# Turning q and k of the first row blocks one tensor at a time, with less MoE work while batch 0 runs

## Chip, cores, metric

One core of a Trainium2 chip. The metric is the device time of one execution, in microseconds (us). A profile gives one execution with a record of every instruction; its span is some 1.8 us shorter than the time of the same execution (352.4 and 354.17 for the profiled execution of the kernel before).

## The reference, cut

Causal attention with a forget gate, 8 batches x 8 heads, 576 rows, head size 64, then a two-layer MoE block (one expert here) with SiLU on the 4608 rows of 512 that come out.

```python
def _attn_ref(q, k, v, f):                     # q, k, v: (8, 8, 576, 64); f: (8, 8, 576)
    scores = scale * np.matmul(q, k.transpose(0, 1, 3, 2))
    cum = np.cumsum(np.log(np.clip(f, 0.0001, 1.0)), axis=-1)
    decay = cum[:, :, :, None] - cum[:, :, None, :]
    scores = np.where(causal, -1000000000.0, scores + decay)
    ...                                        # softmax
    return np.matmul(attn, v)

def _moe_ref(x, w_in, w_out):                  # x: (4608, 512), w_in: (512, 2048), w_out: (2048, 512)
    h = x @ w_in
    g = h * (1.0 / (1.0 + np.exp(-h)))
    return (g @ w_out).astype(np.float32)
```

## The kernel before

The first 128 rows of each of the 8 batches ("blocks 0 to 7") are done first, since each needs only its own 128 keys. Blocks 0 to 3 form MoE group 0 (512 rows), blocks 4 and 5 group 1, blocks 6 and 7 group 2 (256 rows each). Then comes the loop over the remaining rows: batch 0, batch 1 and so on, each in four units of two heads; two units make a "pair". ( `u` below is the exponential of a unit's scores, `ut` that of its tail, the last 64 rows.) Program order is the order of issue on every engine.

A block is turned (q and k transposed by matmuls into PSUM, q evacuated by the scalar engine, ACT, and k by the vector engine, DVE), scored, masked, multiplied with v, normalised and turned back:

```python
    def load_qk0(b):
        t = conv.tile([P, 2, RUN * D], BF16, name="qkb", tag="qkb")     # conv: 4 buffers
        for i, src in enumerate((q, k)):
            nc.gpsimd.dma_start(out=t[:, i, :], in_=src[b, :, 0:P, :].rearrange(...))
        qk0[b] = t

    def turn0(b, between=0):
        src = qk0.pop(b)
        qT0[b] = qktp.tile([P, NP, P], BF16, name="qkT", tag="qkT")
        for i, (dst, evac) in enumerate(
            ((qT0[b], nc.scalar.copy), (kT0[b], nc.vector.tensor_copy))
        ):
            ...                       # 16 matmuls into tp, then evac(dst, tp)
```

For the remaining rows the software engine (POOL) casts a loaded unit to bf16, and a transposing DMA turns it.

```python
    def cast_qk(n):
        b, p = divmod(n, NP)
        t2 = conv.tile([P, NX, 2 * D], BF16, name="qkb", tag="qkb")
        ...                           # three POOL casts
        qbf[n] = t2

    def transposes(n):
        src = qbf.pop(n)
        t = qktp.tile([P, NX, P], BF16, name="qkT", tag="qkT")
        ...
        nc.sync.dma_start_transpose(out=t[:, :, :], in_=src[:, :, :].rearrange("p x c -> p (x c)"))
```

MoE work lies between all this in pieces: `m1_chunk` (first layer: four matmuls, a tanh on ACT, a product `gt` on DVE) and `m2_part` (second layer: four matmuls of 512 columns; the last part of a row block sends its output by the sync queue). `fill` issues pieces until a budget is spent; what it overdraws is carried in `at["left"]` to the next call. `least` is a minimum number of pieces whatever the account says.

```python
    def fill(us_, first=0, least=0):
        ...
        at["left"] += us_ * 1000
        while at["left"] > 0 or least > 0:
            t = step()                # one chunk or one part; returns its estimated ns
            if t is None:
                at["left"] = 0.0
                return False
            at["left"] -= t
            least -= 1
        return True

    def two_more(b):
        turn0(b)
        fill(0.6, 0, 1)
        turn0(b + 1)
        fill(0.6, 0, 1)
        scores0(b)
        mask0(b)
        fill(0.6, 2, 1)
        ...

    fill(4.0)
    two_more(4)
    ready.add(1)
    fill(6.0)
    open2["w"] = True                 # the second layer may begin
    fill(5.0, 2)
    two_more(6)
    ready.add(2)
    fill(1.0, 2)

    def prepare(n):                   # issues on the sync queue (SP) and on POOL
        if n + 4 < NU:
            load_qk(n + 4)
        if n + 2 < NU:
            cast_qk(n + 2)
            transposes(n + 2)
        ...                           # v of the next batch

    for m in range(NQ):
        n = 2 * m
        piece = 1.4 if m < 2 else 2.4
        scores(n, 0)
        scores(n, 1)
        prepare(n)
        slot(piece, 2)                # = fill(piece, 2) and some bookkeeping
        ...
        attend(n)
        attend(n + 1)
        slot(min(3.5, max(0.8, behind() - LAG)), 1)
```

The softmax here doesn't subtract the row's maximum and nothing guards it: scores larger than these inputs give would overflow.

## Time and profile before

| what | value |
|---|---|
| time, median of 3 (later 4) | 354.05 (354.06) us, 353.91 to 354.12 |
| tensor engine (PE) idle in the span | 15.6 us of 352.4 |
| PE waiting on transposed q and k | none among the ten largest waits |
| first MoE matmul | 20.65 us |
| first chunk of group 1 | 40.45 us |
| batch 0 begins | 61.12 us |

The three times of the lower rows are starts of matmuls in the PE timeline; I use them as mile marks. A change that removes idle time moves the later marks forward, if the work before them is the same; where it isn't, its duration has to be taken off first (four matmuls of 512 columns are 0.865 us, four of 256 are 0.44).

### The profile page before, as it was taken

To read this page: it belongs to the slowest core of one execution; us is meant where nothing else is said; L and a number is where in the kernel's file an instruction comes from. 1 tells how busy PE (TensorE), PEld (TensorE's weight loads), DVE (VectorE), ACT (ScalarE), POOL (GpSimd) and SP (SyncE) were. 2 spreads that over 40 slices of the span, in tenths; PEclk is the share of its full clock that TensorE was granted. 3 is DMA by queue.
4 is the path that set the end of the run, shared out by engine and by line. 5 is a ranking of instruction groups with operands and counts; after the bars stand their busy time and mean duration, and the time that the engine had idled before them with its cause. 6 is when DMAs were issued, how large, how long until landed. Compare 5 with 4: busy or idle time off the path is not lost.

```text
span 352.4 us, 8990 instructions
## 1 busy us (share of the span) xinstructions
PE 336.8 (96%) x3598; PEld 203.7 (58%) x3646; DVE 188.8 (54%) x409; ACT 218.3 (62%) x399; POOL 103.2 (29%) x183
## 2 busy tenths in 40 slices
PE   7888988999899999999999999999999999999995
PEld 3544554666656566565665666756566565555664
DVE  4566824456566465656656546646556544444340
ACT  5555716785766867759658675676856744444341
POOL 6992146254062144127017115412600000000000
PEclk9999999999999999999999999999999999999999
DMA  8999999998865795699279389848722000010012
GB/s 159 215 200 201 196 192 196 213 211 182 188 135 110 184 206 120 105 209 197 74 150 230 75 186 211 169 99 183 159 58 58 32 32 30 30 61 31 32 60 60
DMA packets 138969, 47.92 MB, mean 136 GB/s; under 512 B 127984, under 2 KB 134384, under 8 KB 138928
## 3 DMA queue, kind: packets, MB, share of 16 engines
q1 hardware_dynamic: 132240, 40.93, 55.9%
q0 software_dynamic: 6528, 6.29, 10.8%
q8 instruction: 28, 0.46, 0.5%
q10 hardware_dynamic: 160, 0.13, 0.1%
q14 instruction: 13, 0.11, 0.1%
HBM read 36.85 MB, written 9.44 MB: 131 GB/s over the span
## 4 chain that ended last, share of the span: by engine, by line
PE 89%; ACT 3%; DVE 2%; issue 2%; DMA 2%; POOL 1%; POOLq 0%; ACTq 0%
PE po L570 35%; PE hp L532 34%; PE sc L433 7%; PE dn L478 5%; PE dn L487 3%; PE tx L508 2%; DMA qkb<-in_k_dram 2%; PE tp L271 2%; ACT u L312 1%; DVE gt L541 1%; ACT u L437 1%; POOL qkb L124 1%; DVE xq L350 1%; ACT th L540 1%; PE sc L305 1%
## 5 line engine op out<-in xcount | busy, mean ns | idle before, releaser
L541 DVE SCALAR_TENSOR_TENSOR gt<-th,hp 128x384 bf16<-128x384 bf16 (+2 forms) x208 | 106.0, 522 | 79.8 <-ACT th L540 76.5
L540 ACT ACTIVATE th<-hp 128x384 bf16<-128x384 f32 (+2 forms) x208 | 95.5, 475 | 85.7 <-PE hp L532 82.9
L532 PE MATMUL hp<-x,w_in_bf 128*128 128x384 bf16 (+2 forms) x829 | 145.9, 314 | 2.6 <-DVE gt L541 0.8
L570 PE MATMUL po<-w_out_bf,gt 128*128 128x512 bf16 (+1 forms) x550 | 139.3, 374 | 3.2 <-issue 1.6
L532 PEld LDWEIGHTS <-w_in_bf 128*128 128x128 bf16 x832 | 78.9, 98 | 56.6 <-issue 3.2
L570 PEld LDWEIGHTS <-gt 128*128 128x128 bf16 x592 | 54.2, 98 | 48.7 <-issue 2.5
L437 ACT ACTIVATE u<-sc 128x1024 bf16<-128x1024 f32 (+1 forms) x96 | 74.6, 814 | 10.7 <-PE sc L433 10.1
L387 POOL TENSOR_TENSOR vp<-vf,w_bf 128x520 bf16<-128x520 f32 (+1 forms) x32 | 34.0, 1063 | 45.3 <-DMA vf<-in_v_dram 43.0
L442 DVE TENSOR_TENSOR u<-u,tri 128x768 bf16<-128x768 bf16 x32 | 21.8, 681 | 22.5 <-ACT u L437 22.5
L373 POOL CAST qkb<-qf 128x384 bf16<-128x384 f32 x32 | 17.1, 535 | 54.7 <-DMA qf<-in_q_dram 49.9
L579 ACT ACTIVATE osb<-po 128x512 f32<-128x512 f32 (+1 forms) x37 | 22.0, 593 | 16.2 <-PE po L570 15.8
L456 DVE TENSOR_TENSOR ut<-ut,trit 128x128 bf16<-128x128 bf16 x32 | 9.3, 291 | 33.3 <-ACT ut L449 33.3
L433 PE MATMUL sc<-qkT 64*128 64x128 bf16 (+1 forms) x640 | 26.5, 207 | 0.1
L433 PEld LDWEIGHTS <-qkT 64*128 64x128 bf16 x640 | 18.2, 94 | 8.8 <-issue 5.8
L449 ACT ACTIVATE ut<-sc 128x640 bf16<-128x640 f32 x32 | 22.8, 714 | 0.0
L478 PEld LDWEIGHTS <-u 128*128 128x128 bf16 x576 | 20.7, 97 | 2.7 <-issue 0.2
L478 PE MATMUL dn<-vp,u 128*128 128x65 bf16 x384 | 21.8, 194 | 0.0
L496 DVE TENSOR_TENSOR xr<-dn,rec 128x448 bf16<-128x448 f32 x32 | 20.0, 624 | 1.1
L373 POOL CAST qkb<-kf 128x384 bf16<-128x384 f32 x32 | 16.6, 519 | 11.5 <-DMA kf<-in_k_dram 11.3
L478 PE MATMUL dn<-v,u 128*128 128x65 bf16 x192 | 19.8, 194 | 0.0
L377 POOL CAST qkb<-qktf 128x128 bf16<-128x128 f32 x32 | 10.6, 333 | 21.3 <-DMA qktf<-in_k_dram 21.3
L433 PE MATMUL sc<-qkT,kT 64*128 64x64 bf16 (+1 forms) x128 | 16.0, 258 | 0.0
(64 smaller groups left out, 191.1 us busy)
## 6 DMA issues: line engine op xcount, KB each, us to landing
vf<-in_v_dram SPq DMA_DIRECT2D x32, 256.0 KB, 4.9
out_dram<-osb SPq DMA_DIRECT2D x32, 256.0 KB, 2.3
qf<-in_q_dram SPq DMA_DIRECT2D x64, 96.0 KB, 2.9
kf<-in_k_dram SPq DMA_DIRECT2D x64, 96.0 KB, 2.7
w_in_bf<-in_moe_w_in_dram POOLq DMA_DIRECT2D x4, 512.0 KB, 9.9
w_out_bf<-in_moe_w_out_dram POOLq DMA_DIRECT2D x4, 512.0 KB, 13.5
qkb<-in_q_dram POOLq DMA_DIRECT2D x8, 128.0 KB, 7.1
qkb<-in_k_dram POOLq DMA_DIRECT2D x8, 128.0 KB, 7.4
```

What stands on the lines that cost most here:

```text
L373: nc.gpsimd.tensor_copy(out=t2[:, c0 : c0 + NR, :].rearrange("p c x -> p (c x)"), in_=t[:, :, :, :].rearrange("p c h d -> p (c h d)"),)
L387: nc.gpsimd.tensor_tensor(out=vbf[b][r, c, :, :], in0=vst[b][c][r, :, :], in1=w_bf[r, c + 1, b * H : (b + 1) * H, None].to_broadcast([n, H ...
L433: nc.tensor.matmul(sc[:, i, o : o + q1 - q0], lhsT=kt, rhs=t[r, q0:q1], start=True, stop=True)
L437: nc.scalar.activation(out=u[:, :, c * SM : c * SM + w], in_=sc[:, :, 0:w], func=ACT.Exp, scale=scale)
L442: nc.vector.tensor_tensor(out=x, in0=x, in1=tri[:, None, None, :].to_broadcast([P, 2, NR, P]), op=ALU.mult,)
L449: nc.scalar.activation(out=ut[:, :, 0:3:2, :].rearrange("p k i t -> p i k t"), in_=sc[:, :, T0 : T0 + (NM + 1) * ST].rearrange("p i (k t) ...
L478: nc.tensor.matmul(dn[:, i * NR + c - 1, :], lhsT=u[:, i, o : o + P], rhs=vals(kb, i), start=(kb == 0), stop=(kb == c),)
L532: nc.tensor.matmul(hp[:, :], lhsT=w_in_bf[:, cc, fc * P : (fc + 1) * P], rhs=xg(g)[:, cc, :], start=(cc == 0), stop=(cc == NCC - 1),)
L540: nc.scalar.activation(out=th[:, :], in_=hp[:, :], func=ACT.Tanh, scale=0.5)
L541: nc.vector.scalar_tensor_tensor(out=gt[:, fc, :], in0=th[:, :], scalar=1.0, in1=hp[:, :], op0=ALU.add, op1=ALU.mult,)
L570: nc.tensor.matmul(po[:, :], lhsT=gt[:, fc, tb * P : (tb + 1) * P], rhs=w_out_bf[:, fc, m0:m1], start=(fc == 0), stop=(fc == NFC - 1),)
L579: nc.scalar.activation(out=osb[:, :], in_=po[:, :], func=ACT.Copy, scale=0.5)
```

## The change

Its intent: start the MoE work earlier by filling the first twenty microseconds better (turn one tensor at a time, hold v of blocks 2 and 3 back behind k of block 0, finish block 3 in two halves), lay more chunks beside blocks 6 and 7, and in exchange put less MoE work into batch 0.

```diff
-    for b in range(4):
-        load_v0(b)
+    load_v0(0)
+    load_v0(1)
+    after(qk0[0][0:1, 1, 0:16])        # the sync queue waits for k of block 0
+    load_v0(2)
+    load_v0(3)
...
-    def turn0(b, between=0):           # both tensors
-        src = qk0.pop(b)
+    def turn0(b, i):                   # one tensor
+        src = qk0[b]
...                                     # out0 and back0 can work in halves
-    turn0(1)
-    sc = ban0(0)
-    scores0(0, sc)
-    turn0(2)
-    sc = ban0(1)
-    scores0(1, sc)
+    turn0(1, 0)
+    turn0(1, 1)
+    scores0(0, ban0(0))
+    scores0(1, ban0(1))
...
-    keep_warm(2)
-    out0(3)
-    back0(2, on_dve)
-    keep_warm(2)
-    back0(3, on_act)
+    keep_warm(1)
+    out0(3, 1)
+    back0(2, on_act)
+    back0(3, on_act, on_dve)
...
     def two_more(b):
-        turn0(b)
-        fill(0.6, 0, 1)
-        turn0(b + 1)
-        fill(0.6, 0, 1)
+        for x in range(2):
+            for i in range(2):
+                turn0(b + x, i)
+                fill(0.3, 0, x == 1 or i == 1)
...
-        fill(1.6, 2, 1)
+        fill(2.4, 2, 3)
...
-        fill(0.8, 0, 1)
+        fill(0.8, 0, 2)
...
-    fill(5.0, 2)
+    fill(3.0, 2)
     two_more(6)
     ready.add(2)
-    fill(1.0, 2)
...
-    LAG = 12.0
+    LAG = 13.0
...
-        piece = 1.4 if m < 2 else 2.4
+        piece = 1.3 if m < 2 else 2.4
...
-        slot(min(3.5, max(0.8, behind() - LAG)), 1)
+        slot(min(3.5, max(0.8, behind() - LAG)) if m > 1 else 0.8, 1)
```

More of the change, by code (lines that the diff above doesn't have):

```diff
@@ L258 @@
     u0: dict[int, bass.AP] = {}
-    def turn0(b, between=0):
-        src = qk0.pop(b)
-        qT0[b] = qktp.tile([P, NP, P], BF16, name="qkT", tag="qkT")
-        for i, (dst, evac) in enumerate(
-            ((qT0[b], nc.scalar.copy), (kT0[b], nc.vector.tensor_copy))
-        ):
-            if i == 1 and between:
-                keep_warm(between)
-            tp = pbig.tile([P, NP, NRUN, RUN], FP32, name="tp", tag="big")
-            for c in range(RUN):
-                for j in range(2):
-                    nc.tensor.matmul(
-                        tp[j * D : (j + 1) * D, :, :, c].rearrange("p a r -> p (a r)"),
-                        lhsT=src[:, i, c * D : (c + 1) * D],
-                        rhs=sel[:, j, :],
-                        start=True,
-                        stop=True,
-                    )
-            evac(
-                out=dst[:, :, :].rearrange("p a t -> p (a t)"),
-                in_=tp[:, :, :, :].rearrange("p a r c -> p (a r c)"),
-            )
+    def turn0(b, i):
+        src = qk0[b]
+        if i == 0:
+            qT0[b] = qktp.tile([P, NP, P], BF16, name="qkT", tag="qkT")
+        dst, evac = ((qT0[b], nc.scalar.copy), (kT0[b], nc.vector.tensor_copy))[i]
+        tp = pbig.tile([P, NP, NRUN, RUN], FP32, name="tp", tag="big")
+        for c in range(RUN):
+            for j in range(2):
+                nc.tensor.matmul(
+                    tp[j * D : (j + 1) * D, :, :, c].rearrange("p a r -> p (a r)"),
+                    lhsT=src[:, i, c * D : (c + 1) * D],
+                    rhs=sel[:, j, :],
+                    start=True,
+                    stop=True,
+                )
+        evac(
+            out=dst[:, :, :].rearrange("p a t -> p (a t)"),
+            in_=tp[:, :, :, :].rearrange("p a r c -> p (a r c)"),
+        )
     def ban0(b):
@@ L333, with out0 @@
     xqs: dict[int, bass.AP] = {}
-    def out0(b):
+    def out0(b, step_=2):
         dn = psc.tile([P, 2, 4, P], FP32, name="dn0", tag="sc")
@@ L349, in out0, with back0 @@
         xq = xqp.tile([P, H, D], BF16, name="xq", tag="xq")
-        nc.vector.tensor_tensor(
-            out=xq[:, :, :].rearrange("p (g j) d -> p g j d", g=2),
-            in0=dn[:, :, :, 0:D],
-            in1=rec[:, :, :, None].to_broadcast([P, 2, 4, D]),
-            op=ALU.mult,
-        )
+        for g in range(0, 2, step_):
+            nc.vector.tensor_tensor(
+                out=xq[:, 4 * g : 4 * (g + step_), :].rearrange("p (g j) d -> p g j d", j=4),
+                in0=dn[:, g : g + step_, :, 0:D],
+                in1=rec[:, g : g + step_, :, None].to_broadcast([P, step_, 4, D]),
+                op=ALU.mult,
+            )
         xqs[b] = xq
-    def back0(b, copy):
+    def back0(b, *copies):
         xq = xqs.pop(b)[:, :, :].rearrange("p (c j) d -> p c (j d)", j=2)
-        tx = pbig.tile([P, NCC, P], BF16, name="tx", tag="big")
-        for cc in range(NCC):
-            nc.tensor.transpose(tx[:, cc, :], xq[:, cc, :], ident_bf[:, :])
         g, c0 = HEADS_OF[b]
-        copy(out=xg(g)[:, :, c0 : c0 + P], in_=tx[:, :, :])
+        k = NCC // len(copies)
+        for n, copy in enumerate(copies):
+            tx = pbig.tile([P, k, P], BF16, name="tx", tag="big")
+            for cc in range(k):
+                nc.tensor.transpose(tx[:, cc, :], xq[:, n * k + cc, :], ident_bf[:, :])
+            copy(out=xg(g)[:, n * k : (n + 1) * k, c0 : c0 + P], in_=tx[:, :, :])
     def cast_qk(n):
@@ L649 @@
     weights_scan()
-    turn0(0, between=3)
+    turn0(0, 0)
+    keep_warm(3)
+    turn0(0, 1)
     nc.vector.tensor_scalar(
@@ L672 @@
     load_v0(4)
+    turn0(2, 0)
+    turn0(2, 1)
     out0(0)
-    turn0(3)
-    sc = ban0(2)
-    scores0(2, sc)
+    turn0(3, 0)
+    scores0(2, ban0(2))
     convert_v0(2)
     load_v0(5)
+    turn0(3, 1)
     out0(1)
     back0(0, on_dve)
-    sc = ban0(3)
-    scores0(3, sc)
+    scores0(3, ban0(3))
     convert_v0(3)
```

## The prediction

> **What bounds the kernel now.** I read the page first (engine shares, the chain that ended last), then the tensor engine's busy time stage by stage, then what it waited for, then the order of instructions of both built programs on each engine.
>
> ```profile
> span 352.4 us, 8990 instructions
> PE 336.8 (96%) x3598; PEld 203.7 (58%) x3646; DVE 188.8 (54%) x409; ACT 218.3 (62%) x399; POOL 103.2 (29%) x183
> PE 89%; ACT 3%; DVE 2%; issue 2%; DMA 2%; POOL 1%; POOLq 0%; ACTq 0%
> ```
>
> The tensor engine is busy for 336.8 of 352.4 us and no other engine passes 62%. The change removes three warm-up matmuls and no other tensor work, so the time can only move by what happens to the 15.6 us in which that engine stands idle. Where they lie, stage by stage (first column the stretch, second its length, third the tensor engine's busy time):
>
> ```profile
> 0.00:20.60 20.60, 16.32 (x235) 9.36 (x239) 10.58 (x25) 11.26 (x14) 17.37 (x42) 1.00 1.09 188
> 20.60:40.40 19.80, 18.45 (x167) 8.97 (x170) 13.58 (x23) 12.72 (x22) 9.21 (x13) 1.00 1.23 200
> 40.40:61.10 20.70, 18.52 (x190) 11.22 (x190) 9.88 (x21) 9.56 (x20) 9.50 (x15) 1.00 1.08 195
> 61.10:69.30 8.20, 7.78 (x128) 5.19 (x130) 2.84 (x8) 6.67 (x11) 2.30 (x5) 1.00 0.88 212
> 84.40:100.70 16.30, 15.36 (x182) 10.14 (x183) 8.82 (x23) 10.66 (x21) 4.90 (x9) 1.00 0.88 187
> 100.70:340.00 239.30, 237.03 (x2464) 142.95 (x2495) 131.19 (x286) 154.13 (x284) 52.53 (x90) 1.00 0.53 115
> 340.00:352.40 12.40, 8.51 (x61) 5.79 (x60) 1.54 (x4) 3.01 (x7) 0.00 (x0) 1.00 0.23 64
> ```
>
> Idle is 4.3 us before the first MoE matmul (1.2 of it the start), 1.35 while blocks 4 and 5 run, 2.2 while 6 and 7 run, 0.4 in the first pair of batch 0 (61.1 to 69.3), 0.9 in the third (a wait of 0.8 at 91.4), 2.3 over the next 239 us, 3.9 after the last matmul. The change touches the first five: at most about 8 us, 2% of the time. What those idle times wait for:
>
> ```profile
> PE dn L340 <- DVE u L321: 1.5, 3, 0.6
> PE hp L532 <- DVE kT L278: 0.8, 1, 0.8
> PE hp L532 <- ACT x L364: 0.7, 1, 0.7
> PE tp L271 <- DMA qkb<-in_q_dram: 0.6, 1, 0.6
> PE tp L271 <- DMA qkb<-in_k_dram: 0.5, 2, 0.4
> PE tx L362 <- DVE xq L350: 0.5, 2, 0.4
> PE sc L286 <- ACT u L312: 0.5, 1, 0.5
> ```
>
> These are latencies of masks, evacuations and loads with too little tensor work laid beside them. The DMA share is above 1 in every slice up to 61 us.
>
> **What the Trainium skill says.** "TensorE: Matmul & The Clock Gate", Back-to-back issue gap: a warm matmul of N columns takes N/2.4 + 2.5 ns, 216 ns for 512. The trace agrees: the first 20 of 512 columns take 4.48 us with the drain of the last. So I count 0.865 us for four of 512 columns and 0.44 for four of 256. The same page, Why this matters for your kernels, wants no idle gap over about 3 us lest the clock fall. The longest single wait here is 1.2 us and the granted clock is 1.00 in these stages; the pauses that I expect below are about 1 us each, so I count no clock loss, also not from three fewer warm-ups. "DMA: Bandwidth & Descriptors", Queues, rings and completion order: each DMA engine takes turns between its queues. The trace agrees: from 9 to 12 us the software queue (q, k, weights) moved 0.45 MB while the hardware queue (v) moved 0.15. Holding v back can therefore only re-order a saturated stream. "Perfetto Trace Analysis", Optimization Strategy, advises interleaving regimes with different limits; the change does so more in one place and less in another.
>
> **The change part by part.** I carry durations of the trace through the new order: turning one tensor (16 matmuls) 0.51 us, exponential of a block about 1.0, evacuation of q 0.58 and of k 0.69, mask 0.69, reciprocal and product 0.9.
>
> *Held v.* By 7 us the hardware queue has moved 0.67 MB, which is f, v of block 0 and of block 1; blocks 2 and 3 had hardly begun when k of block 0 landed (6.75). So q0, k0 and q1 (8.4) gain nothing; q2 and k2 come perhaps 0.8 us earlier, v2 and v3 some 0.3 later.
>
> *The first four blocks.* The exponential of block 1 no longer waits behind turning block 2: it starts at about 11.5 and not 12.76. Carried on, the exponential of block 3 starts at about 16.0 (17.04), the last product is split in halves, and the first MoE matmul starts at about 19.0 (20.65): 1.65 us, with 0.65 of warm-up matmuls in it. The first quarter of the input weights has landed by then (18.3).
>
> *Blocks 4 and 5.* Here most of it is lost again. q of block 5 lands at about 26.6 (issued 16.75, 9.8 to landing), and the stream is saturated, so it does not come earlier. The tensor engine would be there at 25.3: it waits 1.3. The next MoE chunk takes the PSUM bank of that q, whose evacuation must wait for the scores of block 4 (only one buffer for it is free): 0.6. Six chunks later the sixteenth is done before block 5 comes back, so nothing lies beside its copy: 0.7 more. Against that, the two mask waits (0.7) vanish. The first chunk of group 1 starts at about 39.9 instead of 40.45: 0.5 us ahead.
>
> *Blocks 6 and 7.* Three chunks instead of two lie between masks and outputs, two between outputs and turning back, and single tensors are turned between chunks, in banks that the built program gives free in time. All 2.1 us of waits should go. Other small gaps: 0.5. In all the tensor engine is some 3.1 us ahead in work when batch 0 begins.
>
> *The first pair of batch 0.* Counting chunks in the built orders, the kernel after has by then done 5 first-layer chunks of 256 (2.2 us) and 4 second-layer parts (3.5 us) more. The minimum counts of the fills overdraw their account by 4.1 us, so the first pair gets no chunk at all among its scores and attention (4 parts and 2 chunks before, 4.3 us). What is left there is 3.7 us of tensor work, against the scalar engine's 0.5 for an output plus 5.7 for exponentials (two pairs of 0.95 each, and 0.27 + 0.6 for each tail). With two score buffers the tensor engine follows it: about 7.0 us for 3.7 of work, a loss of 3.3, in pauses of about 1 us; 3.2 net of the 0.1 before.
>
> *The third pair.* Five first-layer chunks in a row cost 0.8 us before because the second layer had run out. After, chunks and parts alternate there: 0.8 gained.
>
> *Transposed q and k.* The third output DMA now stands in the sync queue ahead of the loads of block 4. It is ready about 1.3 us after batch 0 begins, and the queue was contiguous before:
>
> ```profile
> 60.76 1.70 SPq L583 DMA_DIRECT2D out_dram<-osb  x2
> 62.51 1.04 SPq L150 DMA_DIRECT2D qf<-in_q_dram  x2
> ...
> 78.22 1.25 SPq L401 DMA_TRANSPOSE qkT<-qkb  x1
> ```
>
> From the loads at 62.5 to the transpose at 78.2 it needs 15.2 us without the two outputs between, and 3.2 to landing. It would land 18 to 20 us after the batch's start; the third pair now comes after 7.0 + 0.9 + 9.4 = 17.3. That is a wait of 0.7 to 2.5 unless the freer stream speeds the issues (v loads took 1.0 us each here, 0.75 at 94 us). I enter 0.7.
>
> Sum: -3.1 + 3.2 - 0.8 + 0.7 = 0.0. The tuning of such small constants was probably judged by measurements, so I shade it a little down: 353.8 us.
>
> **Rivals.** (1) The earlier start is kept: the wait on q5 is smaller, since by 9 us more of the software queue is done, and pauses in the first pair are filled better than I think: 350.5 to 352. For it: q5's landing is read from another mix of traffic. Against it: the saturated share. (2) The transposes bind: third pair, then the second half of it wait, 2 to 3 us: 356. For it: the contiguous sync queue. Against it: the loads had spare time in later pairs. (3) The overdrawn account costs nothing, because the scalar engine runs ahead: 350.5. Against it: two score buffers and 5.7 us of exponentials in 7 us.
>
> **Range and chances.** Each of the four terms may be off by about 1 us: two in the root of squares. So 351.6 to 356.0. Faster by over 2% would need 7.1 us, nearly all idle that the change can touch; slower by over 2% a new wait of that size, or the clock falling. 0.02 each.
>
> **What would show it.** Right: first MoE matmul near 19.0; a wait of the turning on the q5 load near 25; idle of blocks 6 and 7 under 0.7 us; no MoE matmul between the first scores and the end of the first pair's attention, with about 3 us idle and score matmuls waiting for exponentials; the 0.8 us wait in the third pair gone; the rest unchanged. Wrong: the first pair takes much less than 7 us, or scores wait over 2 us for transposes, or the granted clock is under 1.00 after it.

## More of the kernel before

The recorded texts also write "pair 4" or "pairs 0 and 1" of loads and casts where they mean units; their "first pair" and "third pair" are two units each.

The builder (the library that allocates the buffers and sets the semaphores) picks the actual SBUF buffer of every tile that shares a tag.

## The result

The kernel after took 358.98 us (median of 4, 358.71 to 359.80); the kernel before, beside it, 354.06 (353.91 to 354.12). The ratio is 1.0143 (95% interval 1.0125 to 1.0161). A ratio here is the mean time of one kernel's fast runs over that of the other's of the same rounds, so not quite the ratio of the medians. It is slower by 4.9 us: within 2%, but outside the range that I gave (351.6 to 356.0).

The page of the kernel after, engine shares and the chain that ended last:

```profile
PE 341.4 (96%) x3643; PEld 205.0 (57%) x3643; DVE 186.0 (52%) x410; ACT 218.8 (61%) x400; POOL 103.0 (29%) x183
PE 87%; DMA 6%; DVE 1%; SPq 1%; ACT 1%; POOL 1%; issue 1%; POOLq 0%; ACTq 0%
```

The tensor engine's share is the same 96%, which says nothing. (Its busy time is 4.6 us more with less work: about 1% of the matmul records of the kernel before are missing, 3598 of them being there for 3646 weight loads, so I work with mile marks and waits, not with the sums.) The chain says more: transfers hold 6% of it instead of 2%, and the sync queue (SPq) appears. The stages of the kernel after, cut at its own mile marks (stretch, length, PE busy, weight loads, DVE, ACT, POOL, granted clock, DMA share, GB/s):

```profile
0.00:19.25 19.25, 17.24 (x235) 9.60 (x236) 10.18 (x26) 11.48 (x15) 15.76 (x35) 1.00 1.07 188
19.25:41.20 21.95, 18.62 (x168) 9.24 (x168) 14.43 (x25) 13.14 (x22) 10.87 (x19) 1.00 1.23 200
41.20:66.10 24.90, 24.64 (x230) 14.99 (x229) 12.05 (x25) 11.31 (x24) 10.30 (x16) 1.00 0.86 160
66.10:73.80 7.70, 5.03 (x109) 3.52 (x110) 3.18 (x8) 6.01 (x9) 1.92 (x5) 1.00 0.90 234
...
84.00:100.00 16.00, 13.27 (x179) 9.67 (x179) 7.67 (x22) 10.56 (x22) 4.64 (x10) 1.00 0.86 166
100.00:344.50 244.50, 244.50 (x2524) 145.76 (x2523) 131.30 (x290) 155.81 (x289) 54.89 (x93) 1.00 0.54 117
```

Idle is 3.3 us in the second stretch, 0.3 in the third, 2.7 in the fourth, 2.7 in the one from 84 us, and none from 100 to 344.5 us. What the tensor engine waited for in the kernel after (in total, times, longest):

```profile
PE sc L436 <- DMA qkT<-qkb: 3.5, 2, 2.7
PE sc L436 <- ACT u L440: 2.1, 3, 1.1
...
PE tp L271 <- DMA qkb<-in_q_dram: 1.0, 1, 1.0
PE sc L305 <- DVE kT L278: 0.8, 1, 0.8
PE hp L535 <- ACT qkT L278: 0.7, 1, 0.7
```

The first line is new and the largest: score matmuls of batch 0 wait for transposed q and k. The second is the first pair, where nothing lies beside the exponentials. The other three are blocks 4 and 5.

With the mile marks of both traces the 4.9 us come apart as follows (minus is gained):

| stage | how it is worked out | us |
|---|---|---|
| up to the first MoE matmul | 19.25 - 20.65 | -1.4 |
| to the first chunk of group 1 | (41.21 - 19.25) - (40.45 - 20.65) | +2.2 |
| to the start of batch 0 | (66.09 - 41.21) - (61.12 - 40.45), less 5.65 of more work (5 chunks of 256, 4 parts) | -1.5 |
| first pair, without its MoE work | (72.84 - 66.09) - (69.27 - 61.12 - 4.34) | +2.9 |
| waits for transposes | 0.77 at 77.28 and 2.73 at 86.75, none before | +3.5 |
| third pair's wait on `gt` | 0.84 before, gone | -0.8 |
| sum | | +4.9 |

The two profiled executions themselves differ by 4.5 us (spans of 356.9 and 352.4), so 0.4 us of this sum is made up elsewhere; I can't say where.

**Why the transposes are late.** The two waits stand before unit 3, the second half of the second pair, and before unit 4, the start of the third pair:

```profile
77.28 0.40 PE L436 MATMUL sc<-qkT 64*128 64x128 bf16 x8 [0.77 <-DMA qkT<-qkb]
86.75 0.40 PE L436 MATMUL sc<-qkT 64*128 64x128 bf16 x8 [2.73 <-DMA qkT<-qkb]
```

In the kernel before the third pair starts without a wait:

```profile
84.44 0.40 PE L433 MATMUL sc<-qkT 64*128 64x128 bf16 x8
```

The sync queue of the kernel after (start, duration, what it does; a row that is long holds back all below it):

```profile
54.27 6.47 SPq L404 DMA_TRANSPOSE qkT<-qkb  x2
...
65.09 2.06 SPq L586 DMA_DIRECT2D out_dram<-osb  x3
67.20 1.24 SPq L150 DMA_DIRECT2D qf<-in_q_dram  x2
...
82.07 1.44 SPq L404 DMA_TRANSPOSE qkT<-qkb  x1
```

and its first row in the kernel before:

```profile
54.23 2.85 SPq L401 DMA_TRANSPOSE qkT<-qkb  x2
```

The transposes of units 0 and 1 start at the same moment, but the second one is issued 3.6 us later (6.47 for both instead of 2.85). The loads of unit 4 start at 67.20 instead of 62.51, and the transpose that the third pair needs at 82.07 instead of 78.22; whether the one follows from the other is tested below. (Counted from the start of batch 0 these loads are no later than before: 1.1 us after it, and 1.4 before. What moved is when the third pair is due: 17.9 us after that start, and 23.3 before, since it has less MoE work ahead of it. A queue that is held can't go ahead of the batch to make up for that.)

The reason for the 6.47 us stands on POOL, in the cast of unit 1 (start, duration, then the idle time before it and what ended it), here in the kernel after:

```profile
57.82 0.51 POOL L376 CAST qkb<-qf 128x384 bf16<-128x384 f32 x1 [8.27 <-DMA qkT<-qkb]
```

and here in the kernel before:

```profile
49.88 0.51 POOL L373 CAST qkb<-qf 128x384 bf16<-128x384 f32 x1 [0.42 <-DMA qf<-in_q_dram]
```

Before, that cast waits for its data. After, it waits 8.27 us for a transpose, which makes no sense as data: the cast *feeds* a transpose. It is a buffer that must come free. In the built programs (the addresses are in no trace) the casts of units 0 and 1 write to SBUF addresses 110496 and 116640 in the kernel before, and both to 110496 in the kernel after. So unit 1 can't be cast before unit 0 has been transposed. The diff does not touch these lines, nor the number of buffers (4); the builder made another choice.

**Blocks 4 and 5.** The two engines that evacuate them, in the kernel after. First ACT, the copy of q of block 5 and what it waited for:

```profile
30.30 0.59 ACT L278 CAST qkT<-tp 128x512 bf16<-128x512 f32 x1 [3.96 <-PE sc L305]
```

Then DVE, the copy of k of block 5 and the product ahead of it:

```profile
31.42 0.69 DVE L544 SCALAR_TENSOR_TENSOR gt<-th,hp 128x512 bf16<-128x512 bf16 x1 [4.36 <-ACT th L543]
32.03 0.68 DVE L278 CAST kT<-tp 128x512 bf16<-128x512 f32 x1
```

The copy of q must wait for the scores of block 4, whose buffer it takes; the tanh behind it on ACT waits with it; the `gt` product on DVE waits for the tanh; and the copy of k stands behind that product in DVE's order. So k waits 4 us for q's buffer, through two engines, though it needs nothing of q. That is the 0.80 us wait at 32.77, beside 1.02 for the load of q5 at 26.73, 0.73 at 30.94 and 0.70 at 41.21.

**The first pair.** The PE timeline of the kernel after (start, duration, and in brackets the idle time before it):

```profile
67.76 0.23 PE L436 MATMUL sc<-qkT 64*128 64x128 bf16 x2 [1.05 <-ACT u L440]
...
70.46 0.23 PE L436 MATMUL sc<-qkT 64*128 64x128 bf16 x2 [0.52 <-ACT u L440]
```

No MoE matmul stands among the scores from 66.09 to 70.78.

### The profile page after: what moved, and what is told of

It reads as the page before. It is cut to its first block, busy times and chain, and to the rows that moved or that the text cites. A ratio compares the mean times of both kernels' runs of the same rounds, so it can differ in the third digit from the quotient of the medians.

```text
span 356.9 us, 9037 instructions
## 1 busy us (share of the span) xinstructions
PE 341.4 (96%) x3643; PEld 205.0 (57%) x3643; DVE 186.0 (52%) x410; ACT 218.8 (61%) x400; POOL 103.0 (29%) x183
## 4 chain that ended last, share of the span: by engine, by line
PE 87%; DMA 6%; DVE 1%; SPq 1%; ACT 1%; POOL 1%; issue 1%; POOLq 0%; ACTq 0%
PE po L573 35%; PE hp L535 32%; PE sc L436 6%; PE dn L481 4%; DMA qkb<-in_q_dram 3%; PE dn L490 2%; PE tp L271 2%; PE tx L511 2%; PE wm L225 2%; DMA qkT<-qkb 1%; DMA vf<-in_v_dram 1%; DMA qf<-in_q_dram 1%; SPq L150 1%; PE sc L305 1%; SPq L404 1%
## 5 line engine op out<-in xcount | busy, mean ns | idle before, releaser
L573 PE MATMUL po<-w_out_bf,gt 128*128 128x512 bf16 (+1 forms) x592 | 146.5, 374 | 0.0
L445 DVE TENSOR_TENSOR u<-u,tri 128x768 bf16<-128x768 bf16 x32 | 19.5, 611 | 30.1 <-ACT u L440 30.1
L436 PEld LDWEIGHTS <-qkT 64*128 64x128 bf16 x640 | 18.4, 94 | 14.7 <-issue 7.7
L459 DVE TENSOR_TENSOR ut<-ut,trit 128x128 bf16<-128x128 bf16 x32 | 7.8, 243 | 30.2 <-ACT ut L452 30.0
```

Source lines behind the costliest of these rows:

```text
L436: nc.tensor.matmul(sc[:, i, o : o + q1 - q0], lhsT=kt, rhs=t[r, q0:q1], start=True, stop=True)
L573: nc.tensor.matmul(po[:, :], lhsT=gt[:, fc, tb * P : (tb + 1) * P], rhs=w_out_bf[:, fc, m0:m1], start=(fc == 0), stop=(fc == NFC - 1),)
```

## The experiments

My theory after reading the traces: the loss is the sum of the table, with two blockers one behind the other in the sync queue, the shared cast buffer and the third output, as the cause of the 3.5 us (A in the expectations). The rivals: the shared buffer alone (B); the third output alone, which I had predicted as the cause of late transposes (C); and the overdrawn account of `fill`, with transposes a consequence. All runs were correct against the reference.

| run | median us (range) | ratio to before | 95% |
|---|---|---|---|
| after | 358.98 (358.71 to 359.80) | 1.0143 | 1.0125 to 1.0161 |
| a_owncast | 358.96 (358.15 to 360.05) | 1.0131 | 1.0107 to 1.0154 |
| a_outact | 361.25 (361.02 to 361.72) | 1.0198 | 1.0181 to 1.0215 |
| a_owncast_outact | 357.17 (356.38 to 358.21) | 1.0080 | 1.0055 to 1.0105 |
| a_nodebt | 356.99 (356.57 to 357.39) | 1.0073 | 1.0058 to 1.0088 |
| b_prologue_only | 354.08 (353.83 to 354.76) | 0.9999 | 0.9986 to 1.0011 |
| b_debt_alone | 358.60 (357.77 to 360.05) | 1.0127 | 1.0104 to 1.0151 |
| b_turn_whole | 359.13 (358.44 to 359.49) | 1.0136 | 1.0122 to 1.0150 |
| b_nodebt_owncast | 356.53 (355.87 to 357.06) | 1.0066 | 1.0050 to 1.0081 |
| c_lateout | 361.04 (360.65 to 362.59) | 1.0198 | 1.0179 to 1.0217 |
| c_owncast_lateout | 356.78 (356.02 to 357.26) | 1.0068 | 1.0054 to 1.0082 |
| c_split45 | 356.76 (356.01 to 356.90) | 1.0065 | 1.0051 to 1.0079 |
| c_mix | 353.96 (353.78 to 354.45) | 0.9991 | 0.9978 to 1.0005 |

The medians of the kernel before in the three sets (a, b, c) were 354.46, 354.23 and 354.36, and 354.06 beside the kernel after. A difference of medians from different sets is therefore uncertain by some 0.4 us; where it matters I give the difference of the ratios too, in us.

### a_owncast: the cast tile gets its own tag

The kernel after, with buffers of their own for the casts, which can then not be shared with the blocks' tiles:

```diff
-        t2 = conv.tile([P, NX, 2 * D], BF16, name="qkb", tag="qkb")
+        t2 = conv.tile([P, NX, 2 * D], BF16, name="qkc", tag="qkc")
```

> The casts of a pair get a pool tag of their own, so that the cast of pair 1 no longer shares its buffer with the cast of pair 0 (8.3 us wait of the GpSimd engine after). Theory A, two blockers one behind the other in the sync queue: the transposes of pairs 0 and 1 go out 3.6 us sooner, but the queue then stands before the third output DMA, which is ready only 0.8 us after batch 0 begins (about 66.9), so the loads of pair 4 start at 67.2 as before and the time stays at 358.5 to 359.5. Rival B, the shared buffer alone makes the 3.5 us of waits for transposes: 355 to 356.

358.96 us, as the kernel after. The sync queue of this run:

```profile
54.63 2.75 SPq L404 DMA_TRANSPOSE qkT<-qkc  x2
...
61.07 6.17 SPq L586 DMA_DIRECT2D out_dram<-osb  x3
67.29 1.01 SPq L150 DMA_DIRECT2D qf<-in_q_dram  x2
```

The transposes take 2.75 us again, so the shared buffer did cause the 6.47. But nothing comes of it in the queue, as the next row shows: the third output is not computed yet, and the queue stands before it until 67.2. The loads of unit 4 start where they did (67.29, 67.20). Two blockers lie one behind the other, and each hides the other. One wait for transposes of 1.4 us is left of the 3.5, but the scores of unit 4 start only 0.8 us earlier (85.96 and 86.75): most of the difference in waits is there because the first pair took longer, so that the third was due later. From its first score to the second pair's first score, the same instructions in the same order, the profiled execution needs 8.92 us (66.18 to 75.10) and that of the kernel after 7.71 (66.09 to 73.80), with the same waits for exponentials. The granted clock fell. The same run by stretches of 2 us (the last figures: clock, DMA share, GB/s):

```profile
68.00:70.00 2.00, 0.99 (x24) 0.57 (x20) 0.61 (x2) 2.00 (x4) 0.00 (x0) 1.00 0.80 208
70.00:72.00 2.00, 1.48 (x39) 1.39 (x37) 0.56 (x1) 2.00 (x4) 1.45 (x3) 0.79 0.93 188
72.00:74.00 2.00, 2.00 (x36) 1.86 (x34) 1.02 (x4) 0.29 (x1) 0.15 (x1) 0.50 0.76 174
```

After some 4 us in which the tensor engine was busy about half (0.95 and 0.99 of 2 us from 66 to 70), its clock is lowered for some three microseconds, to 0.50 from 72 to 74, at a cost of 1.2 us. The profiled execution of the kernel after has the same pauses and a clock of 1.00; its other executions have means of 0.988, 0.988 and 0.998 over the span. So this loss comes in some executions and not in others; in the kernel after it would end in front of a wait for transposes and be partly hidden there, which I have not shown.

### a_outact: the third output from ACT's queue

```diff
-                q_ = nc.scalar if last and n == 1 else nc.sync
+                q_ = nc.scalar if (last and n == 1) or (g == 0 and tb == 2) else nc.sync
```

> The outputs of the third row block of group 0 are sent from the scalar engine's queue, so the sync queue no longer waits for them; the shared cast buffer stays. Theory A: the loads of pair 4 start about 1 us sooner (66.2 against 67.2), the waits for transposes fall from 3.5 to about 2.5 and the time is 357.5 to 358.5. Rival C, the output DMA alone holds the queue: waits nearly gone, 355 to 356.

361.25 us, outside what either theory expected. It says nothing on them: with the shared buffer still there, the output's issue on ACT held that engine, and the tensor engine waited 5.4 us at once for an exponential. The clock then stood at 0.50 for 8 us (70 to 78). Moving a blocked issue to another queue moves the block.

### a_owncast_outact: both

> Both undone. Theory A: loads of pair 4 start near 62.5 to 63.5, the waits for transposes (3.5 us) vanish, 355 to 356. If the transposes were held by DMA bandwidth instead, waits of over 2 us remain and the time stays above 357.

357.17 us, above the 355 to 356 that I expected. The loads of unit 4 start at 63.29 and no matmul waits for transposes, so removing both blockers is enough to remove the 3.5 us of waits. (It isn't the only way: see a_nodebt.) But ACT waits again (the largest wait for `u` is 2.0 us) and the clock is 0.50 from 70 to 76, so of the 3.5 us only 1.8 (358.98 - 357.17; 2.2 by the ratios) show in the time: from the first to the second pair it needs 10.67 us, 3.0 more than the kernel after.

### a_nodebt: the account starts at zero in the loop

The kernel after, with one line ahead of the loop over the pairs:

```diff
+    at["left"] = 0.0
```

> The overdrawn account is set to zero before batch 0, so that the first pair gets MoE chunks again (3 parts, 4 chunks). Theory: the 2.7 us of idle in the first pair go, the waits for transposes stay (about 3.5), and the five chunks in a row in the third pair come back (0.8): 356.5 to 357.5. Rival: the idle only moves to the transposes, since they land at the same time: 358.5 to 359.5.

356.99 us, as expected. The first pair gets chunks among its scores, its waits for exponentials fall from 2.1 to 0.8 us, those for transposes from 3.5 to 1.1 (everything in batch 0 comes later, so the queue has more time), and the wait of 0.8 on `gt` is back. The clock is 1.00. So the overdrawn account is the origin of 2.0 us (2.5 by the ratios), part of it through the transposes. Both blockers are still there in this run, and the loads of unit 4 start as late (67.32). The waits for transposes thus need both: a queue that is held, and a third pair that is due early (19.2 us after the start of batch 0 here, 17.9 in the kernel after).

### b_prologue_only: the change up to the first MoE matmul alone

The kernel before, with the held v, the new order of the first four blocks and the last in halves; blocks 4 to 7, the account and the buffers as before.

```diff
     def two_more(b):
-        turn0(b)
+        turn0(b, 0)
+        turn0(b, 1)
         fill(0.6, 0, 1)
-        turn0(b + 1)
+        turn0(b + 1, 0)
+        turn0(b + 1, 1)
         fill(0.6, 0, 1)
```

> The change up to the first MoE matmul alone (v held, the order of the first four blocks, the halved last block, one warm-up instead of four); from blocks 4 and 5 on everything is as before, and so are all buffers. Theory: the first MoE matmul starts at 19.2 instead of 20.65, but block 5 cannot be turned before its q and k land at 26.6 and 27.3, so 0.2 to 0.6 us of the 1.4 are left: 353.5 to 354.2. Rival: the whole 1.4 us is kept: 352.6.

354.08 us, ratio 0.9999: nothing. The first MoE matmul starts at 19.58 (20.65 before), so 1.1 us are there; the tensor engine then waits 0.49 us for q and 0.28 for k of block 5, where the kernel before waits for neither, and at the scores of block 4 the two kernels are level (28.99 and 29.03). The gain is handed back within 10 us: block 5 can't be turned before 26.53, and my prediction had read from the kernel before that its q lands at about 26.6.

### b_debt_alone: the kernel before with the account overdrawn

```diff
+    at["left"] = -4140.0
     for m in range(NQ):
```

> The kernel before, with its account of MoE work overdrawn by 4.14 us when batch 0 begins, and nothing else: its first pair then gets no chunk among its scores, as after. Theory: 2 to 3 us of idle in the first pair, less the 0.8 us of the five chunks in a row in the third pair: 355.5 to 356.5, perhaps with a lowered granted clock. Rival (idle there is free, as the chunks are only moved): 354.

358.60 us, more than expected. The scores wait 2.3 us for exponentials and 0.5 for the tails. The profiled execution, one of four, also had a slow start (first MoE matmul at 22.90, 2.25 us late, with a mean clock of 0.83 from 10 to 20 us). Over all four executions the account costs 4.5 us by the ratio. The two fastest (357.8) would make it 3.6, but that is a choice of mine: of the two others only one was profiled. Either figure is more than the 2.9 of the first pair in the kernel after, and I can't place the rest.

### b_turn_whole: blocks 4 to 7 turned two tensors at a time

The kernel after, with `two_more` turning both tensors in a row:

```diff
         for x in range(2):
             for i in range(2):
                 turn0(b + x, i)
-                fill(0.3, 0, x == 1 or i == 1)
+            fill(0.6, 0, 1)
```

> The kernel after, but blocks 4 to 7 are turned both tensors in a row with one chunk after them. The built program then gives the casts of pairs 0 and 1 separate buffers again, no output DMA stands ahead of the loads of pair 4 that is not yet ready, and the account is overdrawn by less, so that the first pair gets 3 parts and 1 chunk. Theory: no waits for transposes (3.5 us), no wait of 0.8 for k of block 5 behind a product of the vector engine, 1 us of idle in the first pair: 352.5 to 354.5. Rival, it is the minimum counts and the constants of the main loop that cost: above 356.5.

359.13 us; I had expected 352.5 to 354.5, and this was my worst miss. The rival of that expectation (the minimum counts and constants cost: above 356.5) is what came. The cast buffers are separate again, the account is not overdrawn as far, and batch 0 begins at about 59, because fewer chunks are done before it. Yet the waits for transposes are 4.3 us in four pieces, more than with the shared buffer, and the clock falls to 0.60 and 0.54 (74 to 78). The kernel of this run differs from that of b_prologue_only in budgets, minimum counts and constants of `fill` and of the loop alone. These alone thus cost 5.0 us (359.13 - 354.08), with no split block and no shared buffer: as much as the whole change, and so not to be added to the other parts. My reading is that the pairs come faster than the sync queue can bring q and k (batch 0 begins at 59.35, the loads of unit 4 start at 63.48), so the chunks that the change takes out of batch 0 also paced the loads. Which of the constants does it (LAG, `piece`, the 0.8 in the last slot, the counts) was never tried one by one.

### b_nodebt_owncast: account at zero and own buffers

> The kernel after with the account set to zero and the casts in a pool tag of their own. Theory: neither idle in the first pair nor a wait for transposes of over 0.5 us; what is left against before is the 2.2 us lost in blocks 4 and 5 less the gains: 354.8 to 356. Rival: the transposes still come late (third output DMA ahead of the loads): as with the account alone, 357.

356.53 us, a little above what I expected (354.8 to 356). Waits for transposes are 0.5 us and the clock is 1.00. What is left above the kernel before, about 2.3 us by the ratio, I put down to blocks 4 and 5, where the waits of 1.1, 0.7, 0.8 and 0.7 stand unchanged. That is argued from the trace: the run also keeps the constants of the loop.

### c_lateout: the third output behind the next loads, in the same queue

The kernel after; the issue is held in a list and sent in the pair's code after the loads and transposes of that pair:

```diff
-                q_.dma_start(out=out[...], in_=osb[r, :])
+                if g == 0 and tb == 2:
+                    held.append(send)
+                else:
+                    q_.dma_start(out=send[1], in_=send[2])
```

> The output DMA of the third row block of group 0 stays in the sync queue but is issued after the loads and transposes of pairs 4 and 5, so that no engine waits for it (the run that sent it from the scalar engine held that engine for 5.4 us and tells nothing). The casts still share a buffer. Theory of two blockers one behind the other: loads of pair 4 about 1 us sooner than 67.2, waits for transposes 2.5 instead of 3.5: 358 to 358.7. Rival, the output alone: 355.5.

361.04 us, worse than expected. The sync queue of this run:

```profile
54.50 7.91 SPq L404 DMA_TRANSPOSE qkT<-qkb  x2
...
67.18 1.17 SPq L150 DMA_DIRECT2D qf<-in_q_dram  x2
```

Without the output the loads still start at 67.18: now the shared buffer alone holds the queue, for 7.91 us. This is the mirror of a_owncast. (My expectation, that the loads would start 1 us sooner, was wrong.) The one wait for transposes is 3.4 us, as long as the two of the kernel after, and the clock fell twice in the profiled execution (0.50 from 70 to 72, and again from 88 to 92, after that wait); means over the span are 0.984 to 0.990 in the four. That fits the 2 us beyond the kernel after, but no run separates it.

### c_owncast_lateout: both blockers removed, no work for ACT

> Both blockers gone. Theory: the loads of pair 4 start near 62.5, no wait for transposes of over 0.3 us, the 3 us of idle in the first pair stay: 355 to 356, or up to 2 more in executions in which the granted clock falls there. Rival, the early pairs simply run faster than q and k can be loaded: waits of over 2 us stay, 357.5 or more.

356.78 us. The sync queue of this run:

```profile
55.10 2.75 SPq L404 DMA_TRANSPOSE qkT<-qkc  x2
...
63.59 1.01 SPq L150 DMA_DIRECT2D qf<-in_q_dram  x2
```

The loads start at 63.59 and no matmul waits for transposes. This is the cleanest measure of the two blockers together: 358.98 - 356.78 = 2.2 us (2.7 by the ratios), of 3.5 us of waits that are gone. The first pair's waits stay (2.1 for `u`), and in the profiled execution the clock falls after them (0.74, 0.50 and 0.91 in the three stretches from 70 to 76): first to second pair takes 8.84 us, 1.1 more than in the kernel after, and batch 0 starts 0.3 later (q5 came later). So 3.5 - 1.1 - 0.3 = 2.1, and the two profiled executions do differ by 2.1 (358.71 and 356.61). That holds for these two; one of the other executions had a clock of 1.00 and took 357.26, so the clock is not the only thing that varies.

### c_split45: blocks 4 and 5 one tensor at a time, and nothing else

The change up to the first MoE matmul, and for blocks 4 and 5 alone:

```diff
+        for x in range(2):
+            for i in range(2):
+                turn0(b + x, i)
+                fill(0.3, 0, x == 1 or i == 1)
```

> The order up to the first MoE matmul as after, and of the rest only one thing: blocks 4 and 5 are turned one tensor at a time with a chunk between. Fills and account as before; the build then lets the casts of pairs 0 and 1 share a buffer, as after. Against the prologue alone (354.1): theory, the two waits in blocks 4 and 5 (evacuation of q of block 5, k of block 5 behind a product) cost 1.5 us and the shared buffer alone little: 355.3 to 356. Rival, the shared buffer alone brings the waits for transposes: 357 or more.

356.76 us, 2.7 more than b_prologue_only (2.3 by the ratios), at clock 1.00; I had expected 355.3 to 356. It brings the waits of 0.73 and 0.80 us on the copies of q and k of block 5, as in the kernel after, and 1.4 us of waits for transposes. The built program has the shared cast buffer; that the 1.4 us come from it is not tested here. So this one piece of the change, four lines, loses at blocks 4 and 5 and makes the builder share.

### c_mix: what gained, without what lost

First blocks as after, 4 and 5 as before, 6 and 7 as after, the account at zero, the constants of batch 0 as before, and the fill ahead of blocks 6 and 7 at 4.0 (5.0 before, 3.0 after). Against the kernel before:

```diff
-    two_more(4)
+    two_a(4)                           # as before
...
-    fill(5.0, 2)
-    two_more(6)
+    fill(4.0, 2)
+    two_b(6)                           # as after
...
+    at["left"] = 0.0
```

> A try at something better than both: start as after, blocks 4 and 5 turned and filled as before, blocks 6 and 7 as after (its least counts), the account set to zero before batch 0, constants of the main loop as before. Theory: the 2.1 us of waits in blocks 6 and 7 fall to under 1, nothing else changes: 352.5 to 353.5. If the first pairs then come before their transposes, the gain is lost: 354 to 355.

353.96 us, ratio 0.9991 (0.9978 to 1.0005): the same as before, where I had expected 352.5 to 353.5. My reserve, pairs that come before their transposes, is not the reason: no such wait is among the tensor engine's waits. Its waits for q and k of the first blocks are 2.3 us in all (1.1 before), so part of the gain is lost there. None of the versions beats the kernel before.

## Why the prediction was wrong, point by point

**Wrong: "Transposed q and k ... I enter 0.7".** This step failed most: the term measured 3.5 us, 2.73 before the third pair and 0.77 before the second half of the second. The path was right for the third pair. The third output stood ahead of the loads of unit 4, which started 1.1 us after batch 0 (predicted 1.3); from there to the transpose it took 14.9 us (15.2); the third pair was due at 17.9 (17.3). Only the landing was slow, 4.6 us for 3.2, so the transpose came at 20.7 and not at 18 to 20. The size was chosen badly: out of "0.7 to 2.5" I entered the lowest value, in the hope of faster issues, though my own terms (1.3 + 15.2 + 3.2 - 17.3) make 2.4. (Even the 15.2 is not what its rows give: 78.22 - 62.51, less 1.05 for the two outputs, is 14.7.) The wait in the second pair I did not foresee at all. Nor did I look for the second blocker, the shared cast buffer, which alone holds the queue as long (7.91 in c_lateout): I had the built program and compared the order of instructions, but not the addresses. With both blockers gone no wait for transposes is left (c_owncast_lateout). My second rival had named the result ("The transposes bind: third pair, then the second half of it wait, 2 to 3 us: 356"), with the place of the smaller wait wrong.

**Wrong: "In all the tensor engine is some 3.1 us ahead".** It was 0.7. The first step held: first MoE matmul at 19.25, predicted 19.0. For blocks 4 and 5 I gave back 1.15 (20.65 - 19.0 less the 0.5 that was left) and it was 2.2: the wait for q5 was 1.02 (predicted 1.3), the one for its copy 0.73 (0.6), and the copy's own stall 0.70 (0.7), all near the prediction; most of the missing 1.0 is the 0.80 of k's copy behind the `gt` product. I traced ACT's chain and not what hangs on it on DVE. The sum was off too: 19.0, the 18.45 us of busy time in this stretch before, and the three waits give 40.05 and not 39.9, even if no wait of before is left. For blocks 6 and 7 the idle time is 0.3 us (predicted under 0.7), yet they gained 1.5 and not 2.6 (2.1 of waits and 0.5 for "other small gaps"). Of the 1.1 us between, 0.4 could not be won, since I had counted only 2.2 us of idle there, and 0.3 is the idle that is left; the other 0.4 stays open.

**Right: the first pair.** Predicted a loss of 3.2, measured 2.9, with the exponentials as the waits and no MoE matmul among the scores. a_nodebt and b_debt_alone confirm from both sides that the overdrawn account makes it (2.0 us won by removing it in the one, 3.6 to 4.5 lost by adding it in the other). The numbers differ; other waits change along with it in both runs, and no run separates them.

**Right: the third pair.** The wait of 0.8 is gone, and comes back with a_nodebt.

**Wrong in its form: "so I count no clock loss".** I took the longest single pause (1 us) as what matters. In the runs the clock fell after pauses of at most 1.1 us that together filled half of 4 us. In the three profiled executions in which it did so with the same order of instructions (a_owncast, c_owncast_lateout, c_lateout), the first pair took 0.7 to 1.2 us longer than in the kernel after. The profiled execution of the kernel after had a clock of 1.00 and took 358.71, so it isn't what broke the number; but it took back part of what removing the blockers gained.

**The sum.** Of the 4.9 us of error against 354.0, 2.8 are transposes (3.5 for 0.7) and 2.4 the lost lead (0.7 for 3.1), less 0.3 in the first pair. The shading to 353.8, on the ground that small constants were "probably judged by measurements", had no number behind it. The range failed because I gave each term about 1 us of independent error, when two of them were off by over 2 us to the same side.

**Readings to correct.** "The DMA share is above 1 in every slice up to 61 us" holds for the three stretches shown, not for finer ones (0.58 in the first 5 us, 0.92 from 45 to 50). The "2.3 over the next 239 us" of idle lie where 31 matmul records are missing (2464 for 2495 weight loads) and need not be idle. And the formula for the issue gap stands in the Trainium skill ("TensorE: Matmul & The Clock Gate", Back-to-back issue gap) for a lone matmul; for a stream with a weight load before each, as here, the page gives about 131 ns at 512 columns. The trace has 216 (0.865 us for four), so here the measurement decides for the formula.

**Open.** Which step of the builder's choice makes the buffers coincide: c_split45 shows that splitting blocks 4 and 5 triggers it, b_turn_whole and b_prologue_only that it needs the split, and no run says why. Whether the clock falls in a given execution is not predicted by anything I measured. The last 0.4 us of blocks 6 and 7, the excess of b_debt_alone, and the part of each constant of the loop are not placed.

## What to carry to other kernels

After a reordering, compare the buffers as well as the order: here a wait of a producer on its own consumer's transfer gave a shared buffer away. When something is taken out from between two waits, ask what comes next on the same queue; here two blockers stood in series, and removing either alone gained nothing. Take no size from the low end of your own range without a number for it. And filler between latency-bound steps may be pacing the loads, so taking it away can make a transfer the bound that wasn't one before.

## What the Trainium skill lacked or had wrong

- "TensorE: Matmul & The Clock Gate", Why this matters for your kernels, warns of single idle gaps over about 3 us. No gap was that long in a_owncast before its clock fell: waits of at most 1.1 us, with the tensor engine busy 1.94 of 4 us, were followed by 0.50 from 72 to 74 us. The same page's section on a second failure mode, psum-queue depth-cycling, does tell of frequent micro-idles that make the clock swing, which agrees; what it lacks is how much idle time does it. The runs give one bound: 1.94 of 4 us busy did it in some executions and not in others (1.00 in the profiled one of the kernel after, with 1.88 of 4, and in b_debt_alone after 1.56 of 4, from 64 to 68).
- "DMA: Bandwidth & Descriptors", Queues, rings and completion order, is about what happens after issue. What cost most here comes before it: an issuing engine works in program order and stands still before a transfer whose data or buffer isn't ready (6.17 us before an output, 7.91 before a transpose), with ready loads behind it. I found no page that warns of it.
- "Perfetto Trace Analysis", Optimization Strategy, reads a gap that repeats as a sign of too few buffers. Neither it nor another page that I found covers how to see in a trace that two tiles were given one buffer though four exist. Here the sign was a single wait of 8.27 us of a producer (the cast) on its own consumer's transfer, on an engine that is busy for 29% of the span.
